# Passing the second chunk of MLP columns for batches 0 and 1 before the third: a reordered opening stage in a fused attention, GLU and soft-MoE kernel

## The chip, the cores and the metric

The kernel runs on one core of a Trainium2 chip. The metric is device time in microseconds of one execution; the median of three runs of the kernel before is 681.73 us (680.27 to 682.89). All times below are microseconds unless marked ns. Engines are named as in the profile: PE is TensorE's matmul side, PEld its weight loads, DVE VectorE, ACT ScalarE, POOL GpSimd, SP the engine that issues nearly all transfers.

## What is computed

Eight batches of 512 rows and 32 state rows each go through a cross read, a gated MLP and a soft mixture of experts:

```python
scores = scale * x @ state.T;  xread = softmax(scores) @ state        # per batch and head
scores2 = scale * state @ x.T; sread = softmax(scores2) @ x
y = concat(xread, sread)                                              # 4352 rows of 512 in all
xn = y / sqrt(mean(y*y) + 1e-6) * rms_g
z = (silu(xn @ w_gate) * (xn @ w_val)) @ w_out                        # 1536 columns inside
logits = z @ phi                                                      # 32 slots
slot_in = softmax(logits, over rows).T @ z
out = softmax(logits, over slots) @ experts(slot_in)                  # 8 experts
```

The inner 1536 columns of the MLP are three chunks of 512, numbered 0, 1 and 2 (`c`). The weights `w_gate`, `w_val` and `w_out` arrive as 64-bit floats and are converted on the chip.

## The kernel before, in words

**Units.** The main work is a list of units (g, c, t): batch g, chunk c, tile t of 128 rows. A unit has two slots. In slot 1 PE makes six matmuls of 128x512 into a bank `mm` for the gate (`main_mm`, line 453), ACT takes their SiLU into `sg` (`main_silu`, line 469); in slot 2 PE makes six more for the value, and DVE multiplies the two into `h` (`main_h`, line 474). Ahead of and behind each slot stand the pieces of work that the table `at(u, slot, f, ...)` (line 800 on) puts there. The units of one stage are written out in `stages` (line 777). Stage 0 has sixteen units: batch 0 chunk 0, batch 1 chunk 0, batch 0 chunk 1, batch 0 chunk 2. Stage 1 has eight: batch 1 chunks 1 and 2. From stage 2 on each stage is one batch with its three chunks.

**Weights.** `w_gate` and `w_val` come in half chunks of 1 MB, then `w_out` transposed in six half chunks of 1 MB, each by one transfer that SP issues (`wload`, line 147, tile `raw` or, for every other late one, `raw_t`, which has a single buffer). Each half chunk is converted in two steps. `begin` (lines 172 and 733) is two ACT passes of 1024 columns (lines 184 and 187). `conv1` (lines 192 and 728) is, for each of two halves of 512 columns, three DVE passes (lines 200, 204 and 208) and one POOL addition (line 212), and then the issue of a further load. The results are the tiles `w` (one for each of gate and value and chunk) and `wo`. A table entry of `begin` or `conv1` always takes the next half chunk in the order of loading, so moving an entry moves all that follow.

**Per batch and chunk.** `sw(b, c, gv)` (line 430) multiplies the state of batch b, scaled by `rms_g`, into the converted weights: eight matmuls of 32 output rows into two `misc` banks; ACT copies each bank into `wp` (line 442) and DVE writes the rounding remainder (line 443). The main matmuls of that batch and chunk read this `wp` and the tile `A` of the batch's attention. Three `misc` banks serve all small work in turn, so a group of matmuls waits until the bank used three groups earlier has been read by ACT and DVE. `att_b1` (line 312) uses two of them for the transposes whose copies are `e2T` (line 318); `att_b2` and `att_b3` make the state read of a batch from it (`srd`, `xsT`).

**Output weights.** `wphi_part(c, j)` (line 624) multiplies `phi` with a converted half chunk `wo`; its second half (lines 635 to 639) finishes `wphi` of chunk c. Only then may the `h` tiles of that chunk be turned (`h_T`, line 484, transposes on L109 and a copy to `hT`) and give logits (`lg_mm`, line 494, tile `lg`).

**Order.** Within a slot the framework's scheduler sets the order of instructions on each engine; each engine then runs its own list strictly in that order, and SP issues its transfers in order too, each behind its waits.

Of the kernel before, what the change touches and what calls it, by code (L numbers as in the profile page):

```python
# [20 lines left out]
def kernel(  # L21
# [17 lines left out]
    B, P, H, NT, D = x_n.shape  # L39
# [734 lines left out]
    def rinv(b):  # L774
        rinv_from(b, T[b, "ss"], NT)

    stages = [
        [(g, c, t) for g, c in ((0, 0), (1, 0), (0, 1), (0, 2)) for t in range(NT)],
        [(1, c, t) for c in (1, 2) for t in range(NT)],
    ]  # L780
    for g in range(2, B):
        stages.append([(g, c, t) for c in range(NC) for t in range(NT)])
# [16 lines left out]
    for s, units in enumerate(stages):  # L799
        def at(u, slot, f, *a):  # L800
            plan.setdefault((base + u, slot), []).append((f, a))

        if s == 0:
# [21 lines left out]
            at(3, 1, att_b2, 0)  # L825
            at(5, 1, att_b3, 0)
            at(4, 1, conv1)
            at(6, 2, begin)
            at(6, 1, conv1)
            at(5, 1, sw, 0, 1, 0)  # L830
            at(6, 2, sw, 0, 1, 1)
            at(5, 2, begin)
            at(5, 2, conv1)
            at(7, 2, begin)
            at(8, 1, conv1)
            at(10, 1, att_b1, 1)
            at(9, 1, begin)
            at(6, 2, conv1)
            at(8, 1, begin)
            at(8, 1, conv1)  # L840
            at(10, 2, sw, 0, 2, 0)
            at(10, 2, begin)
            at(11, 1, sw, 0, 2, 1)
            at(12, 2, conv1)
            at(12, 1, wphi_part, 0, 0)
            at(12, 1, begin)
            at(10, 2, conv1)
            at(12, 2, wphi_part, 0, 1)
            at(11, 2, begin)
            at(12, 2, conv1)  # L850
            at(13, 2, wphi_part, 1, 0)
            at(13, 1, sw, 1, 1, 0)
            at(14, 1, begin)
            at(14, 2, conv1)
            at(14, 2, wphi_part, 1, 1)
            at(14, 1, sw, 1, 1, 1)
            at(14, 1, begin)
            at(15, 2, conv1)
            at(15, 2, wphi_part, 2, 0)
            at(11, 2, load_xn, 1)  # L860
# [5 lines left out]
        else:  # L866
            g = s
# [445 lines left out]
```

## Time and profile before

| | us |
|---|---|
| median of 3 runs | 681.73 (680.27 to 682.89) |
| the profiled execution | 679.36 |
| its span | 677.6 |
| PE busy | 635.2 (94%) |
| DVE busy | 405.3 (60%) |
| ACT busy | 388.2 (57%) |
| POOL busy | 131.1 (19%) |
| TensorE's mean granted clock | 0.973 of full speed |

The profile's page gives busy time by engine, the span in 40 slices, the chain of work that ended last, and groups of instructions with what ended their waits. PE holds 74% of the chain that ended last. The trace's timeline of an engine gives, for each run of like instructions, the start, the time from the first start to the last end, the instruction and its tiles (output <- inputs), the count, and in brackets the idle time ahead of it and what ended it. One matmul of float32 data with 32 output rows shows as two records (so `x16` is one `sw` of eight); a main matmul shows as one.

### The profile page before, as it was taken

To read this page: it belongs to the slowest core of one execution; us is meant where nothing else is said; L and a number is where in the kernel's file an instruction comes from. 1 tells how busy PE (TensorE), PEld (TensorE's weight loads), DVE (VectorE), ACT (ScalarE), POOL (GpSimd) and SP (SyncE) were. 2 spreads that over 40 slices of the span, in tenths; PEclk is the share of its full clock that TensorE was granted. 3 is DMA by queue.
4 is the path that set the end of the run, shared out by engine and by line. 5 is a ranking of instruction groups with operands and counts; after the bars stand their busy time and mean duration, and the time that the engine had idled before them with its cause. 6 is when DMAs were issued, how large, how long until landed. Compare 5 with 4: busy or idle time off the path is not lost.

```text
span 677.6 us, 11521 instructions
## 1 busy us (share of the span) xinstructions
PE 635.2 (94%) x4560; PEld 406.8 (60%) x4560; DVE 405.3 (60%) x852; ACT 388.2 (57%) x632; POOL 131.1 (19%) x158
## 2 busy tenths in 40 slices
PE   5789989999999999999999999999999999999980
PEld 4447646456656766666676667666765776753350
DVE  6979996873676368555835773685465366242170
ACT  5467943855786468557755964685445476311170
POOL 2634656230041102010201021011000000002420
PEclk9599979999999999999999999999999999999996
DMA  9950155031042030203110320300091218999858
GB/s 349 405 211 2 60 189 211 38 133 63 1 160 98 5 124 3 98 5 125 36 63 5 121 94 1 122 4 33 13 359 54 73 39 274 314 340 387 324 196 331
DMA packets 33582, 92.56 MB, mean 137 GB/s; under 512 B 1912, under 2 KB 4088, under 8 KB 30712
## 3 DMA queue, kind: packets, MB, share of 16 engines
q1 hardware_dynamic: 33240, 91.76, 37.1%
q8 instruction: 36, 0.59, 0.4%
q14 instruction: 18, 0.15, 0.1%
q10 hardware_dynamic: 288, 0.07, 0.0%
HBM read 79.76 MB, written 12.06 MB: 136 GB/s over the span
## 4 chain that ended last, share of the span: by engine, by line
PE 74%; DVE 8%; ACT 4%; issue 2%; DVEq 0%; POOL 0%; ACTq 0%
PE mm L85 42%; PE misc L85 17%; PE misc L109 10%; PE lg L85 4%; PE so L85 2%; DVE w L200 1%; DVE wp L443 1%; DVE h L479 1%; DVE w L208 1%; ACT L471 1%; ACT L285 1%; DVE wo L208 1%; ACT sg L471 1%; ACT sT L285 0%; DVE w L204 0%
## 5 line engine op out<-in xcount | busy, mean ns | idle before, releaser
L85 PE MATMUL mm<-wp,A 128*128 128x512 f32 x1152 | 310.6, 408 | 0.4 <-DVE h L479 0.4
L85 PEld LDWEIGHTS mm<-wp,A 128*128 128x128 f32 x1152 | 206.4, 190 | 88.0 <-issue 49.1
L479 DVE SCALAR_TENSOR_TENSOR h<-mm,rinv,sg 128x512 f32<-128x512 f32 x102 | 76.0, 747 | 96.0 <-PE mm L85 73.9
L471 ACT ACTIVATE sg<-mm,rinv 128x512 f32<-128x512 f32 x102 | 70.1, 688 | 74.6 <-PE mm L85 68.3
L442 ACT CAST wp<-misc 128x512 fp32r<-128x512 f32 x96 | 51.9, 587 | 65.0 <-PE misc L85 65.0
L443 DVE TENSOR_TENSOR wp<-misc,wp 128x512 fp32r<-128x512 f32 x96 | 62.2, 684 | 41.1 <-ACT wp L442 40.7
L85 PE MATMUL misc<-w,stTg 64*32 64x512 f32 x768 | 70.0, 618 | 9.6 <-POOL w L212 6.0
L490 ACT COPY hT<-misc 128x512 f32<-128x512 f32 x86 | 49.1, 580 | 24.3 <-PE misc L109 20.0
L109 PE MATMUL misc<-ident,h 128*128 128x128 f32 x408 | 60.4, 274 | 1.8 <-DVE h L479 1.4
L109 PEld LDWEIGHTS misc<-ident,h 128*128 128x128 f32 x408 | 48.9, 140 | 16.9 <-DVE h L479 3.4
L308 POOL TENSOR_TENSOR a<-a,asum 128x1024 f32<-128x1024 f32 x7 | 13.4, 1920 | 126.7 <-DVE asum L307 120.5
L471 ACT ACT_TABLE_LOAD x28 | 35.9, 1283 | 3.1 <-PE mm L85 2.7
L85 PEld LDWEIGHTS misc<-w,stTg 64*32 64x32 f32 x768 | 11.7, 106 | 41.3 <-issue 15.7
L416 POOL TENSOR_TENSOR rinv<-ri,rs_magic 128x4 int32<-128x4 int32 (+1 forms) x9 | 1.8, 197 | 173.8 <-DVE ri L412 173.8
L85 PE MATMUL lg<-hT,wphi 128*32 128x512 f32 (+1 forms) x216 | 32.5, 578 | 1.5 <-ACT hT L490 1.5
L212 POOL TENSOR_TENSOR w<-w,raw 128x512 int32<-128x512 int32 x20 | 28.1, 1419 | 27.6 <-ACT wp L442 7.2
L85 PE MATMUL misc<-bd,A 128*128 128x256 f32 x192 | 31.1, 302 | 1.5 <-DVE A L380 1.5
L85 PE MATMUL mm<-wh,xsg 128*128 128x512 f32 x96 | 31.7, 400 | 0.0
L397 ACT ACTIVATE misc<-misc 128x512 f32<-128x512 f32 x32 | 18.8, 586 | 21.7 <-PE misc L85 20.7
L85 PEld LDWEIGHTS misc<-bd,A 128*128 128x128 f32 x192 | 27.2, 202 | 5.8 <-DVE A L380 2.2
L212 POOL TENSOR_TENSOR wo<-wo,raw 128x512 int32<-128x512 int32 x18 | 24.3, 1362 | 28.4 <-DVE wo L208 19.7
L85 PE MATMUL misc<-h,ET 128*32 128x512 f32 x204 | 28.9, 598 | 0.0
(197 smaller groups left out, 828.2 us busy)
## 6 DMA issues: line engine op xcount, KB each, us to landing
ew<-in_w_dram SPq DMA_DIRECT2D x27, 1024.0 KB, 8.3
xT<-in_x_t_dram SPq DMA_DIRECT2D x8, 1024.0 KB, 4.8
xn<-in_x_n_dram SPq DMA_DIRECT2D x8, 1024.0 KB, 6.9
raw<-in_w_val_dram SPq DMA_DIRECT2D x6, 1024.0 KB, 16.6
raw<-in_w_out_dram SPq DMA_DIRECT2D x6, 1024.0 KB, 5.0
out_dram<-ob SPq DMA_DIRECT2D x6, 1024.0 KB, 12.1
ew_w<-in_w_dram SPq DMA_DIRECT2D x5, 1024.0 KB, 10.2
raw<-in_w_gate_dram SPq DMA_DIRECT2D x4, 1024.0 KB, 14.2
```

The lines of the kernel that those rows point to most:

```text
L85: nc.tensor.matmul(out=o, lhsT=lhsT, rhs=rhs, start=start, stop=stop)
L109: nc.tensor.transpose(o, i, ident)
L200: nc.vector.tensor_scalar(out=dst[:, h], in0=dst[:, h], scalar1=EXP_LO, scalar2=EXP_HI, op0=ALU.max, op1=ALU.min,)
L208: nc.vector.scalar_tensor_tensor(out=a[:, h], in0=hi[:, h], scalar=-0x40000000, in1=a[:, h], op0=ALU.bitwise_and, op1=ALU.bitwise_or,)
L212: nc.gpsimd.tensor_tensor(out=a[:, h], in0=a[:, h], in1=rnd[:, h], op=ALU.add)
L308: (eng or nc.gpsimd).tensor_tensor(out=a3, in0=a3, in1=asum.unsqueeze(2).to_broadcast([P, 32, 32]), op=ALU.mult)
L397: nc.scalar.activation(out=ps, in_=ps, func=AF.Square, accum_out=T[b, "ss"][:, t : t + 1])
L442: nc.scalar.copy(t[:, r, 0, :], ps)
L443: nc.vector.tensor_tensor(out=t[:, r, 1, :], in0=ps, in1=t[:, r, 0, :].bitcast(F32), op=ALU.subtract)
L471: nc.scalar.activation(out=sg, in_=ps, func=AF.Silu, scale=RINV[g][:, t : t + 1])
L479: nc.vector.scalar_tensor_tensor(out=HH[g, c][:, t, :], in0=ps, scalar=RINV[g][:, t : t + 1], in1=sg, op0=ALU.mult, op1=ALU.mult,)
L490: (nc.vector.tensor_copy if on_dve else nc.scalar.copy)(HT[g, c][:, :, t * P : (t + 1) * P], ps.rearrange("p (q n) -> p q n", q=4))
```

## The change

The units of stages 0 and 1 change places: chunk 1 is passed by batch 0 and then batch 1 in stage 0, chunk 2 by batch 0 and then batch 1 in stage 1. The number of units of each stage stays, and so does every instruction of the computation. The table of stage 0 is rewritten from unit 6 on: the state products `sw(1, 1, ...)` come in units 10 and 11 and `sw(0, 2, ...)` in units 13 and 14, where they stood the other way round; the conversions of the third chunk and of the transposed output weights, and the parts of `wphi`, come one to three units later. Everything from stage 2 on is written as before.

```diff
     stages = [
-        [(g, c, t) for g, c in ((0, 0), (1, 0), (0, 1), (0, 2)) for t in range(NT)],
-        [(1, c, t) for c in (1, 2) for t in range(NT)],
+        [(g, c, t) for g, c in ((0, 0), (1, 0), (0, 1), (1, 1)) for t in range(NT)],
+        [(g, 2, t) for g in (0, 1) for t in range(NT)],
     ]
...
-            at(10, 2, sw, 0, 2, 0)
...
-            at(12, 1, wphi_part, 0, 0)
...
+            at(10, 2, sw, 1, 1, 0)
...
+            at(13, 1, wphi_part, 0, 0)
+            at(13, 1, sw, 0, 2, 0)
```

Three places show how instructions move. In the names, `w_4` and `w_5` are the converted gate and value of chunk 2, `wp_6` and `wp_7` the state products for gate and value of the unit that follows unit 11 (batch 0 chunk 2 before, batch 1 chunk 1 now), `wo32` a half chunk of output weights; the last numbers of a name differ between the two programs and mean nothing.

**First place: DVE in units 9 to 12.** Before, on DVE:

```order
L208 SCALAR_TENSOR_TENSOR w_5_776<-raw_9_303,w_5_776 128x512 x2
L479 SCALAR_TENSOR_TENSOR h_2_817<-mm_810,rinv_328,sg_786 128x512
L479 SCALAR_TENSOR_TENSOR h_2_817<-mm_831,rinv_328,sg_826 128x512
L318 COPY e2T_848<-misc_849 128x512
L479 SCALAR_TENSOR_TENSOR h_2_817<-mm_861,rinv_328,sg_846 128x512
L443 TENSOR_TENSOR wp_6_869<-misc_870,wp_6_869 128x512
```

Now, on DVE:

```order
L208 SCALAR_TENSOR_TENSOR w_5_794<-raw_8_253,w_5_794 128x512 x2
L318 COPY e2T_833<-misc_834 128x512
L479 SCALAR_TENSOR_TENSOR h_2_792<-mm_848,rinv_328,sg_831 128x512
L200 TENSOR_SCALAR w_5_794<-w_5_794 128x512 x2
L204 TENSOR_SCALAR w_5_794<-w_5_794 128x512
L443 TENSOR_TENSOR wp_6_856<-misc_857,wp_6_856 128x512
L443 TENSOR_TENSOR wp_6_856<-misc_864,wp_6_856 128x512
L208 SCALAR_TENSOR_TENSOR w_5_794<-raw_9_303,w_5_794 128x512
```

The copy to `e2T` now stands ahead of the last half chunk of `w_5` instead of behind it; of that half chunk, three of the five listed passes stand ahead of the remainders of `wp_6`, and the others behind them.

**Second place: PE from unit 12 on.** Before, on PE, with the third chunk's main matmuls of batch 0:

```order
L85 MATMUL mm_940<-wp_6_869,A_0_255 128x512 x6
L85 MATMUL misc_949<-wo32_828,phis_85 32x512 x2
L85 MATMUL mm_992<-wp_7_906,A_0_255 128x512 x6
L85 MATMUL mm_1034<-wp_6_869,A_0_255 128x512 x6
L85 MATMUL mm_1071<-wp_7_906,A_0_255 128x512 x6
```

Now, on PE, the end of unit 15, of batch 1 in chunk 1:

```order
L85 MATMUL misc_1005<-wo32_890,phis_85 32x512 x2
L85 MATMUL misc_1011<-w_4_736,stTg_147 32x512 x4
L85 MATMUL misc_1018<-w_4_736,stTg_147 32x512 x4
L85 MATMUL misc_1043<-wo32_943,phis_85 32x512 x2
L85 MATMUL mm_1127<-wp_6_856,A_1_456 128x512 x4
L85 MATMUL mm_1179<-wp_7_893,A_1_456 128x512 x5
L85 MATMUL misc_1047<-r32_75,wpp_1008 128x32 x4
```

The first product with output weights (`misc<-wo32`) stood inside unit 12; it now stands in unit 15, beside the first use of `w_4`, and the matmuls with `r32` that finish `wphi` of chunk 0 follow the second product as they did.

**Third place: SP's loads of the transposed output weights.** Before, on SP:

```order
L162 DMA raw_t13_757<-in_w_out_t_dram 128x2x1024
L162 DMA raw_10_796<-in_w_out_t_dram 128x2x1024
L162 DMA raw_11_895<-in_w_out_t_dram 128x2x1024
L118 DMA xT_2_923<-in_x_t_dram 128x2048
L162 DMA raw_t15_808<-in_w_out_t_dram 128x2x1024
L126 DMA xn_1_938<-in_x_n_dram 128x2048
L162 DMA raw_12_1029<-in_w_out_t_dram 128x2x1024
L162 DMA raw_t17_1009<-in_w_out_t_dram 128x2x1024
```

Now, on SP:

```order
L162 DMA raw_t13_783<-in_w_out_t_dram 128x2x1024
L162 DMA raw_10_822<-in_w_out_t_dram 128x2x1024
L118 DMA xT_2_910<-in_x_t_dram 128x2048
L126 DMA xn_1_922<-in_x_n_dram 128x2048
L162 DMA raw_t15_888<-in_w_out_t_dram 128x2x1024
L162 DMA raw_11_941<-in_w_out_t_dram 128x2x1024
L162 DMA raw_t17_1033<-in_w_out_t_dram 128x2x1024
L162 DMA raw_12_1101<-in_w_out_t_dram 128x2x1024
```

The loads of `raw_11` and `raw_12` move behind `raw_t15` and `raw_t17`, each of which waits for POOL's last addition on the `raw_t` half chunk before it, since they share one buffer.

## Rows read from the trace of the kernel before

**Rows 1.** The page, busy time of one engine over the span.

```profile
PE 635.2 (94%) x4560; PEld 406.8 (60%) x4560; DVE 405.3 (60%) x852; ACT 388.2 (57%) x632; POOL 131.1 (19%) x158
```

**Rows 2.** Waits of PE from 40 to 260 us: total, times, longest.

```profile
PE misc L85 <- DVE e2T L318: 3.1, 1, 3.1
```

**Rows 3.** Busy time by stretch: stretch, length, PE, PEld, DVE, ACT, POOL, clock, DMA.

```profile
60.00:91.00 31.00, 30.28 (x227) 20.93 (x226) 29.15 (x59) 25.30 (x37) 17.48 (x13) 1.00 0.27 103
...
95.00:101.00 6.00, 6.00 (x24) 3.05 (x19) 5.79 (x13) 1.17 (x2) 2.68 (x2) 0.50 0.01 3
```

**Rows 4.** Timeline of PE around the wait and the units after it.

```profile
75.54 1.07 PE L85 MATMUL misc<-w,stTg 64*32 64x512 f32 x10 [0.21 <-POOL w L212]
76.54 9.82 PE L85 MATMUL mm<-wp,A 128*128 128x512 f32 x42
...
89.79 1.66 PE L85 MATMUL mm<-wp,A 128*128 128x512 f32 x6
94.53 3.10 PE L85 MATMUL misc<-w,stTg 64*32 64x512 f32 x16 [3.08 <-DVE e2T L318]
97.56 4.78 PE L85 MATMUL mm<-wp,A 128*128 128x512 f32 x12
102.26 1.05 PE L85 MATMUL misc<-wo,phis 128*32 128x512 f32 x4
103.25 8.01 PE L85 MATMUL mm<-wp,A 128*128 128x512 f32 x34
```

**Rows 5.** Timeline of DVE, 79 to 109 us.

```profile
79.76 1.29 DVE L200 TENSOR_SCALAR w<-w 128x512 f32<-128x512 f32 x2
...
83.51 2.32 DVE L200 TENSOR_SCALAR w<-w 128x512 f32<-128x512 f32 x2
...
87.63 2.97 DVE L200 TENSOR_SCALAR w<-w 128x512 f32<-128x512 f32 x2
...
91.19 1.28 DVE L208 SCALAR_TENSOR_TENSOR w<-raw,w 128x512 int32<-128x512 int32 x2
...
93.72 0.67 DVE L318 COPY e2T<-misc 128x512 f32<-128x512 f32 x1
...
94.97 0.67 DVE L443 TENSOR_TENSOR wp<-misc,wp 128x512 fp32r<-128x512 f32 x1
...
108.40 0.75 DVE L200 TENSOR_SCALAR wo<-wo 128x512 f32<-128x512 f32 x2
```

**Rows 6.** Timeline of POOL, one pair of additions.

```profile
82.45 3.09 POOL L212 TENSOR_TENSOR w<-w,raw 128x512 int32<-128x512 int32 x2 [2.03 <-ACT sg L471]
```

**Rows 7.** Timeline of SP, and the DMA issues by line (count, size, us to landing).

```profile
80.88 0.98 SPq L162 DMA_DIRECT2D raw<-in_w_out_t_dram  x2
...
101.55 0.37 SPq L162 DMA_DIRECT2D raw_t<-in_w_out_t_dram  x1
...
raw_t<-in_w_out_t_dram SPq DMA_DIRECT2D x3, 1024.0 KB, 5.0
raw<-in_w_out_t_dram SPq DMA_DIRECT2D x3, 1024.0 KB, 8.1
```

**Rows 8.** Timeline of PE at four later points, and two rates.

```profile
115.34 1.08 PE L85 MATMUL misc<-r,wpp 64*128 64x32 f32 x8 [0.39 <-DVE wpp L635]
...
128.04 1.09 PE L109 MATMUL misc<-ident,h 128*128 128x128 f32 x8
...
139.08 1.07 PE L85 MATMUL misc<-r,wpp 64*128 64x32 f32 x8
...
148.13 1.06 PE L85 MATMUL lg<-hT,wphi 128*32 128x512 f32 x8
...
154.22 1.64 PE L85 MATMUL mm<-wp,A 128*128 128x512 f32 x6
```

**Rows 9.** PE before a second wait early on: timeline row, and clock by stretch.

```profile
12.68 1.12 PE L85 MATMUL misc<-w,stTg 64*32 64x512 f32 x4
...
16.00:16.50 0.50, 0.00 (x0) 0.51 1.01 418
```

More of the change, by code (lines that the diff above doesn't have):

```diff
@@ L827 @@
             at(4, 1, conv1)
-            at(6, 2, begin)
-            at(6, 1, conv1)
             at(5, 1, sw, 0, 1, 0)
             at(6, 2, sw, 0, 1, 1)
-            at(5, 2, begin)
             at(5, 2, conv1)
-            at(7, 2, begin)
+            at(6, 2, begin)
+            at(7, 1, conv1)
+            at(7, 1, begin)
             at(8, 1, conv1)
+            at(8, 2, begin)
+            at(9, 2, conv1)
             at(10, 1, att_b1, 1)
[L837 to L840, printed above, removed]
-            at(10, 2, sw, 0, 2, 0)
-            at(10, 2, begin)
-            at(11, 1, sw, 0, 2, 1)
-            at(12, 2, conv1)
-            at(12, 1, wphi_part, 0, 0)
-            at(12, 1, begin)
[L847 to L853, printed above, removed]
+            at(10, 1, begin)
+            at(10, 2, sw, 1, 1, 0)
+            at(11, 1, conv1)
+            at(11, 1, begin)
+            at(11, 1, sw, 1, 1, 1)
+            at(12, 1, conv1)
+            at(12, 1, begin)
+            at(12, 2, begin)
+            at(13, 1, wphi_part, 0, 0)
+            at(13, 1, sw, 0, 2, 0)
+            at(13, 1, conv1)
+            at(13, 2, wphi_part, 0, 1)
+            at(13, 2, begin)
+            at(14, 1, sw, 0, 2, 1)
+            at(14, 1, conv1)
+            at(14, 2, wphi_part, 1, 0)
+            at(14, 2, begin)
             at(14, 2, conv1)
-            at(14, 2, wphi_part, 1, 1)
-            at(14, 1, sw, 1, 1, 1)
-            at(14, 1, begin)
+            at(15, 1, wphi_part, 1, 1)
+            at(15, 1, begin)
             at(15, 2, conv1)
```

## The prediction, made before the change was run

> **What bounds the kernel now.** I began with busy time: PE works 635.2 of 677.6 us [rows 1], so only time in which PE stands still, or runs at its lower clock, can be won. PE's waits show where: between 40 and 260 us one wait stands out, 3.08 us for DVE's copy to `e2T` [rows 2]. PE's timeline places it: the main matmuls end near 91.4, and the `sw` that follows (0, 2, value) begins at 94.53 [rows 4]. The stretches give its cause and its tail. DVE is busy 29.15 of 31 us ahead of it, with the conversion of the third chunk; and from 95 to 101 the granted clock is 0.50, TensorE's 1.2 GHz level [rows 3], after 3.08 us without a matmul. Twelve main matmuls take 4.7 us there, 0.39 each, against 8.01 / 34 = 0.235 afterwards [rows 4]. So about 7 us at most hang on this place: 3.1 of waiting and some 3.5 of slow clock. All else in these stages runs nearly full, with 0.39 us ahead of one `wphi` step [rows 8]. About 0.5% of the time, 3.4 us, is what a measurement of this kernel can tell from no change.
>
> **The change, part by part.** No instruction is added or removed, so the sum is made of waits.
>
> *The first wait moves two groups on.* In the new order only the first half chunk of `w_5` stands ahead of the `e2T` copy. Laid out from where the orders part, that copy ends near 91.5, just as PE arrives. But the second group of the next `sw` needs the bank that the first remainder of `wp_6` frees, and that remainder stands behind three passes of the last half chunk. Before, it ended at 94.97 + 0.67 = 95.64 [rows 5]. Three things shift it:
> - Two L208 and one L204 pass now come after it: 2 x 0.64 from the L208 pair, and 0.38, half of the free L200 pair, which L204 equals [rows 5]: -1.65.
> - DVE now reaches the remainders of `wp_5` with no conversion ahead of them. Their second group's matmuls run from 75.54 to 76.61 [rows 4], ACT's copies come behind those, and ACT's passes for the next half chunk behind the copies. DVE, which had no pause here, stands still about 2.1 (bounds 0, if something fills it, and 3.1, the longest wait that PE's rows show): +2.1.
> - L200 takes 0.75 for a pair when POOL is idle, and 1.29, 2.32 and 2.97 when a pair of POOL's additions (3.09 [rows 6]) is under way [rows 5]. With a fourth pair like the first that is 4.9 over the free price. Now one pair starts with POOL idle, and three start some 1.1 before POOL ends: 3.4. That gives -1.5.
>
> Sum -1.05: the remainder ends near 94.6, and PE resumes at about 94.8, having done four of the eight `sw` matmuls and waited 2.2 in place of 3.08. Its next main matmuls start at 94.8 + 1.07 = 95.9 where they started at 97.56 [rows 4]: **1.65 ahead**, if the clock stays up.
>
> The L200 rows ask for a rule. The pair begun at 83.51 ends at 85.83, 0.3 after the POOL pair that began before it [rows 5, 6]. The Trainium skill (SBUF — State Buffer, "Who interferes with whom") says that VectorE in a two-port mode and GpSimd hold a shared port pair exclusively, whichever issues first, and the other blocks fully; the rows agree. Were the two engines independent, the three pairs would cost 0.75 each, the remainder would come 3 us sooner, the wait of 2.2 would close and the sum would be 679.3; by the rule it is the one below. I take the blocked price because three rows of three show it.
>
> *A second wait opens at unit 12.* The remainders of `wp_7` stand behind three L208, three L204 and two L200 passes (1.9 + 1.1 + 0.75 = 3.8) that follow `wp_6`'s second remainder (95.3). With 0.9 for POOL in the way (between 0 and 2.2, the dearest pair [rows 5]) the first `wp_7` remainder ends near 100.7. PE gets through the `sw` and twelve matmuls by 98.7, issues one of the next six and waits until 100.9: **2.0 us** (1.1 to 3.3). Before, that point of unit 12 was passed at 103.25 + 0.23, so the change is 2.5 ahead. But the first output-weight product, 1.05 [rows 4], was done by then and is now still to come: **1.5 ahead**. So DVE, not the clock, now sets this stretch; most of what the slow clock cost is spent again as waiting.
>
> *The output weights.* Two of the first three half chunks were issued as a pair at 80.88 and landed long before use; `raw_t15` went at 101.55 [rows 7]. Now `raw_11` stands behind `raw_t15`, which waits for POOL's last addition on the first half chunk, whose last L208 stands behind `wp_7`: near 104.1. It lands 5.0 later [rows 7], at 109.2 (8.1, the other rows' landing, is the upper bound). ACT's two passes then hold up its copies for `wp_8`, and the `wphi` sum on DVE ends near 115.0. PE waits about 1.0 and reaches the `r32` step at 115.1, against 115.34 [rows 8]. By then it has also done one `sw` and a transpose that before came later, 1.3 together: still **1.5 ahead**. At the same place the covers go: conversions that ran 3 to 20 us ahead of their products now end as PE arrives. Every product waits for POOL's addition just behind DVE's last pass, and one L208 stands behind the `wphi` copy of the chunk before. By the order I count waits of 1.4, 1.0, 2.2, 0.8, 1.3 and 0.6 up to the last `r32` step, which PE reaches near 140.6 against 139.08 [rows 8]. It has then done 15 more main matmuls (3.5) and eight fewer transposes and four fewer logits matmuls (about 1.85 by [rows 8]; a group of eight transposes or four logits matmuls is 1.06 to 1.09): 1.65 more work, so only **0.1 ahead**.
>
> *Until the orders meet.* `xn_1`, `xT_2` and `xT_3` have 5 us and more in hand after the move. ACT swaps its tables once more in this stretch, beside PE's matmuls; I cost that at nothing; if the SiLUs behind a swap came due, it is in the 1 either way below. The next stage's first main matmuls of batch 1 chunk 2 I place at 151.6 with 2.45 of small work left over, 154.05 against 154.22 [rows 8]. From there the lists carry the same work, and I take 0, with 1 either way.
>
> **Sum:** 0.2 less, on a profiled execution of 679.36. That execution is 2.4 below the median of 681.73; the difference is laid on the median: **681.5 us**.
>
> **The rivals.**
>
> *The hole closes (faster).* If DVE comes to `wp_6` by 92.3 and to `wp_7` by 98.7, 2 us sooner than I count, nothing waits, the clock stays at 2.4 GHz, and what remains to pay is only the output weights' 1.4. For it: each of my DVE terms has bounds of that size, and the conversion does come later. Against it: DVE's queue still holds all four half chunks' passes but two. Price: 3.08 + 3.5 for the hole, less 1.4: 676.5; without that 1.4, 675.2.
>
> *The clock falls twice (slower).* Near 13.8 the `sw` matmuls end and the granted clock is 0.51 by 16.0 [rows 9]: 2.2 us without a matmul sufficed there. So the wait for `wp_6` (2.2) and the wait for `wp_7` (2.0) may each put PE down to 1.2 GHz. The first fall is nearly free, since DVE sets the next stop anyway (0.7). The second falls on unit 12 to 15, which DVE does not hold, and costs 3.5 as the fall before did. It decides at the wait for `wp_7`, whose upper bound is 3.3. Price: 681.5 + 4.2 = 685.7. Against it: four `sw` matmuls split the first wait, and 2.0 is shorter than what both rows show. The Trainium skill (TensorE: Matmul & The Clock Gate, "HAM oscillation — how this bites in real kernels") says that waits between bursts put the clock down again each time, which speaks for this rival; that the single wait of before cost one fall agrees.
>
> *Late loads (slower).* If `raw_t15` and `raw_t17` land after 8.1 instead of 5.0 [rows 7], ACT's strict order holds SiLUs and copies behind them, twice 3.1 less the 2 us of slack that I left: 4.2 more, 685.7.
>
> *The change does nothing (same).* If the scheduler had kept `e2T` behind the conversion, the time would stay at 681.7; the order shows that it did not.
>
> **How the numbers follow.** My forecast, that the wait moves and the output weights give back the rest, gets 0.5. The closed hole gets 0.24, the double fall 0.15, late loads 0.09, and no effect 0.02, which adds to same. So faster 0.24, same 0.52, slower 0.24. The forecast's own range by its bounds (wait for `wp_7` 1.1 to 3.3, pause 0 to 3.1, one either way at the end) is 679 to 684. To leave out no more than 2 in 10 it reaches to the closed hole that still pays for the output weights and to both slow cases: **676.5 to 686**.
>
> **What would show it.** Right: no wait of PE on `e2T` worth naming; a wait of about 2 us on DVE `wp` L443 near 93 and another near 100; a granted clock that stays at 1.00 from 91 to 104; PE waits on POOL `wo` L212 and on DVE `wpp` and `wphi` adding up to 5 to 8 us between 115 and 140; the issue of `raw_t15` near 104. Wrong: PE without waits over 1 us from 91 to 104 (the closed hole), a clock of 0.50 in that stretch or behind it (the double fall), or an ACT wait on the transfer to `raw_t` of more than 4 us (late loads).

## The result, and the profile after

The changed kernel takes **686.15 us** (median of 5 runs, 685.64 to 686.43) against 681.0 for the kernel before in the same session (5 runs): a ratio of **1.0087 [1.0071, 1.0103]**, so slower by 5 to 6 us. The forecast was 681.5, no change that could be told, with a range to 686.0. The profiled execution took 685.64 for a span of 683.8, where before had 677.6, so the two traces differ by 6.2; before's is one of its faster executions (679.36, median 681.0).

The page's busy time of one engine (answers [rows 1]): PE works 3 us more, which no added work explains.

```profile
PE 638.3 (93%) x4560; PEld 405.1 (59%) x4560; DVE 409.3 (60%) x854; ACT 390.8 (57%) x632; POOL 128.0 (19%) x158
```

PE's waits from 40 to 280 us (answers [rows 2]; columns: total, times, longest):

```profile
PE misc L85 <- DVE wp L443: 2.3, 1, 2.3
PE misc L85 <- POOL wo L212: 2.2, 3, 1.5
...
PE misc L85 <- DVE e2T L318: 0.5, 1, 0.5
```

The wait for `e2T` shrank from 3.1 to 0.5 and one for `wp` took its place, as forecast. The waits for POOL's `wo` are new; the forecast had them, and larger. The stretches (answer [rows 3]; columns as there):

```profile
91.00:95.00 4.00, 1.30 (x10) 0.15 (x8) 4.00 (x7) 3.26 (x5) 2.52 (x2) 0.91 0.77 268
95.00:101.00 6.00, 5.87 (x18) 3.34 (x18) 5.96 (x10) 0.59 (x1) 2.76 (x2) 0.50 0.40 164
...
116.00:140.00 24.00, 21.55 (x124) 10.96 (x124) 19.58 (x38) 15.46 (x23) 8.39 (x7) 1.00 0.24 88
```

From 95 to 101 the clock is 0.50, as before. From 116 to 140 PE stands still 2.45 us, where before had 0.29 (11.77 + 11.94 busy in the two halves of that stretch). PE's timeline (answers [rows 4] and [rows 8]):

```profile
91.76 1.06 PE L85 MATMUL misc<-w,stTg 64*32 64x512 f32 x8 [0.52 <-DVE e2T L318]
95.13 1.93 PE L85 MATMUL misc<-w,stTg 64*32 64x512 f32 x8 [2.31 <-DVE wp L443]
...
116.36 1.07 PE L85 MATMUL misc<-r,wpp 64*128 64x32 f32 x8 [0.28 <-DVE wpp L635]
...
119.77 1.05 PE L85 MATMUL misc<-wo,phis 128*32 128x512 f32 x4
...
122.61 1.05 PE L85 MATMUL misc<-wo,phis 128*32 128x512 f32 x2
...
126.11 1.43 PE L85 MATMUL mm<-wp,A 128*128 128x512 f32 x5
...
127.46 1.07 PE L85 MATMUL misc<-r,wpp 64*128 64x32 f32 x8
...
131.03 1.04 PE L85 MATMUL misc<-wo,phis 128*32 128x512 f32 x2 [1.47 <-POOL wo L212]
...
132.94 1.05 PE L85 MATMUL misc<-wo,phis 128*32 128x512 f32 x2 [0.21 <-POOL wo L212]
...
137.56 1.05 PE L85 MATMUL misc<-wo,phis 128*32 128x512 f32 x2 [0.49 <-POOL wo L212]
...
142.15 1.04 PE L85 MATMUL misc<-wo,phis 128*32 128x512 f32 x2
...
144.95 1.08 PE L85 MATMUL misc<-r,wpp 64*128 64x32 f32 x8
...
156.66 1.65 PE L85 MATMUL mm<-wp,A 128*128 128x512 f32 x6
```

Two things are to be seen. First, a product of the output weights that stands whole (x4, at 119.77) takes 1.05; cut in two (x2 and x2, at 131.03 and 132.94, and at 137.56 and 142.15) each half takes as long as the whole, 1.04 to 1.05, and from the start of one to the next row on PE pass 0.97 or 0.98. That is about 1 us for each of these two. A third product is cut together with the logits matmuls beside it: from 122.61 to 126.11 the two take 3.50. In before they took 1.84 (122.54 to 124.38), and one product alone ran long, 2.03:

```profile
122.54 1.07 PE L85 MATMUL lg<-hT,wphi 128*32 128x512 f32 x8
123.42 1.03 PE L85 MATMUL misc<-wo,phis 128*32 128x512 f32 x4
124.38 2.56 PE L85 MATMUL mm<-wp,A 128*128 128x512 f32 x9
...
135.06 2.03 PE L85 MATMUL misc<-wo,phis 128*32 128x512 f32 x4
```

The cuts are busy time, and no view of waits shows them. Second, how the halves come about, in the changed kernel's rows of DVE and POOL behind the `r32` step of 127.46:

```profile
128.57 0.29 DVE L639 COPY wphi<-misc 128x128 f32<-128x128 f32 x1 [1.83 <-PE misc L85]
128.78 0.68 DVE L208 SCALAR_TENSOR_TENSOR wo<-raw_t,wo 128x512 int32<-128x512 int32 x1
```

```profile
129.69 1.28 POOL L212 TENSOR_TENSOR wo<-wo,raw_t 128x512 int32<-128x512 int32 x1 [5.48 <-PE misc L85]
131.60 1.29 POOL L212 TENSOR_TENSOR wo<-wo,raw_t 128x512 int32<-128x512 int32 x1 [0.63 <-DVE wo L208]
```

PE's `r32` step releases DVE's copy, which had kept DVE still for 1.83; behind it in DVE's order stands the L208 pass of the next half chunk, behind that POOL's addition, and behind that PE's product, which starts at 131.03 after 1.47 of waiting. (The row names PE's step as what ended POOL's idle time; the addition reads what L208 wrote, and that ended at 129.46.) PE waits for work that waited for PE.

Where the 6.2 us arise, by the prediction's places: at the first `r32` step (116.36) the kernel was about 0.3 ahead (1.02 later, with 1.3 more work done); at the last (144.95) 4.2 behind (5.87 later, 1.65 more done); at unit 20 (156.66, with 2.45 of work left over) 4.9 behind; at the end 6.2.

### The profile page after: what moved, and what is told of

Read it like the earlier page. It is cut to its first block, busy times and chain, and to the rows that moved or that the text cites. A ratio compares the mean times of both kernels' runs of the same rounds, so it can differ in the third digit from the quotient of the medians.

```text
span 683.8 us, 11523 instructions
## 1 busy us (share of the span) xinstructions
PE 638.3 (93%) x4560; PEld 405.1 (59%) x4560; DVE 409.3 (60%) x854; ACT 390.8 (57%) x632; POOL 128.0 (19%) x158
## 4 chain that ended last, share of the span: by engine, by line
PE 73%; ACT 6%; DVE 6%; issue 2%; POOL 1%; DVEq 0%; ACTq 0%; POOLq 0%
PE mm L85 41%; PE misc L85 17%; PE misc L109 9%; PE lg L85 4%; PE so L85 2%; ACT L471 1%; DVE w L200 1%; ACT L285 1%; ACT sg L471 1%; ACT sT L285 1%; DVE wp L443 1%; DVE wo L208 1%; ACT hT L490 1%; DVE h L479 1%; ACT wp L442 0%
## 5 line engine op out<-in xcount | busy, mean ns | idle before, releaser
L479 DVE SCALAR_TENSOR_TENSOR h<-mm,rinv,sg 128x512 f32<-128x512 f32 x102 | 75.8, 745 | 91.7 <-PE mm L85 73.9
L443 DVE TENSOR_TENSOR wp<-misc,wp 128x512 fp32r<-128x512 f32 x96 | 62.5, 684 | 41.0 <-ACT wp L442 40.4
## 6 DMA issues: line engine op xcount, KB each, us to landing
raw<-in_w_gate_dram SPq DMA_DIRECT2D x4, 1024.0 KB, 14.2
```

What stands on the lines that cost most here:

```text
L443: nc.vector.tensor_tensor(out=t[:, r, 1, :], in0=ps, in1=t[:, r, 0, :].bitcast(F32), op=ALU.subtract)
L479: nc.vector.scalar_tensor_tensor(out=HH[g, c][:, t, :], in0=ps, scalar=RINV[g][:, t : t + 1], in1=sg, op0=ALU.mult, op1=ALU.mult,)
```

## The experiments

The traces do not start alike. The fourth `h` pass (DVE L479), ahead of everything that any edit moves, begins at 61.83 in before and in the changed kernel, but between 61.70 and 63.68 in the others. A single span is therefore compared after taking that difference off. That is the last column. For two kernels there is a second trace (order_timed, late_wo_timed); by it the column would read +1.2 and about +6 instead of +0.6 and +5.5, so it is good to some 0.6 us.

| run | span | fourth `h` | against before |
|---|---|---|---|
| before | 677.6 | 61.83 | 0 |
| the change | 683.8 | 61.83 | +6.2 |
| order_alone | 678.3 | 61.98 | +0.6 |
| late_wo_alone | 684.5 | 63.21 | +5.5 |
| early_wo | 685.9 | 61.94 | +8.2 |
| early_wo_xn | 685.6 | 61.81 | +8.0 |
| products_later | 679.6 | 62.31 | +1.5 |
| pool_whole | 687.0 | 61.80 | +9.4 |
| late_products | 683.5 | 61.98 | +5.8 |
| late_products_b3 | 680.6 | 61.82 | +3.0 |
| wp_first | 684.0 | 61.77 | +6.5 |
| begin8_later | 689.1 | 61.79 | +11.5 |
| both_later | 680.1 | 61.92 | +2.4 |
| both_later_b3 | 682.1 | 63.42 | +2.9 |
| both_latest_b3 | 684.1 | 61.76 | +6.6 |
| before_e2t_act | 679.5 | 62.87 | +0.9 |
| order_e2t | 680.5 | 63.68 | +1.0 |
| before_e2t_pool | 682.0 | 61.70 | +4.5 |

### Which half of the change costs

**order_alone** takes before's table and changes the order of units and the two pairs of `sw` alone:

```diff
-        [(g, c, t) for g, c in ((0, 0), (1, 0), (0, 1), (0, 2)) for t in range(NT)],
-        [(1, c, t) for c in (1, 2) for t in range(NT)],
+        [(g, c, t) for g, c in ((0, 0), (1, 0), (0, 1), (1, 1)) for t in range(NT)],
+        [(g, 2, t) for g in (0, 1) for t in range(NT)],
...
-            at(10, 2, sw, 0, 2, 0)
+            at(10, 2, sw, 1, 1, 0)
```

> Part 1 of the change alone: the units and the two pairs of scaled weights change places, every conversion and every product of the output weights stays at the unit where the kernel before has it. Theory W (the 6.2 us come from the later conversions): span 676.5 to 678.5, as before's 677.6, and the last r32 step near 139 to 140. Theory O (they come from the new order of the units itself): span 682.5 to 684.5 as after's 683.8.

**late_wo_alone** keeps before's order and its conversions of the gate and value columns, and moves the output weights alone:

```diff
-            at(12, 2, conv1)
-            at(12, 1, wphi_part, 0, 0)
+            at(12, 1, conv1)
...
+            at(13, 1, wphi_part, 0, 0)
...
-            at(14, 2, wphi_part, 1, 1)
...
+            at(15, 1, wphi_part, 1, 1)
```

> The kernel before with its order of units and its conversions of the gate and value columns, but with the six output-weight conversions, their beginnings and their products at the units where the change has them. Theory W: the loss of the stretch 116 to 145 comes here too, 3.5 to 5 us, span 681 to 683, and TensorE again waits some 2 us for POOL wo. Theory O: span 677 to 678.5.

The section on the change says that these pieces come one to three units later. For the output weights the table moves less: the first three conversions come half a unit to one and a half later and the first four products half a unit to one, while the last three conversions and the last two products keep their slots and only their beginnings come later.

Measured: +0.6 and +5.5, together 6.1 of the change's 6.2; the second is a little over what theory W gave. Both were timed again, in five rounds each.

> The new order of units with before's conversions and products, timed in five rounds beside the kernel before. By the traces 0.55 us over before when the starts are made equal: ratio 1.000 to 1.002. If the order has a larger part that the single trace hid: 1.003 or more.

> Before's order with the output weights' conversions and products where the change has them, timed in five rounds. By the traces 5.5 us over before when the starts are made equal: ratio 1.007 to 1.009. If one trace overstated it: 1.005 or less.

Ratios: **1.0009 [0.9998, 1.002]** for the order, **1.0075 [1.0062, 1.0087]** for the late output weights. Theory W is shown, theory O falls: the order of units is worth nothing that a measurement can tell, the later output weights are the loss. The two PE timelines show it too; first late_wo_alone, with the change's halves and waits, then order_alone, with before's one cut product:

```profile
132.63 1.04 PE L85 MATMUL misc<-wo,phis 128*32 128x512 f32 x2 [1.47 <-POOL wo L212]
134.55 1.05 PE L85 MATMUL misc<-wo,phis 128*32 128x512 f32 x2 [0.22 <-POOL wo L212]
139.16 1.04 PE L85 MATMUL misc<-wo,phis 128*32 128x512 f32 x2 [0.48 <-POOL wo L212]
143.77 1.04 PE L85 MATMUL misc<-wo,phis 128*32 128x512 f32 x2
146.57 1.08 PE L85 MATMUL misc<-r,wpp 64*128 64x32 f32 x8
```

```profile
134.94 2.03 PE L85 MATMUL misc<-wo,phis 128*32 128x512 f32 x4
...
138.95 1.07 PE L85 MATMUL misc<-r,wpp 64*128 64x32 f32 x8
```

### What in the late output weights costs

**early_wo** is the changed kernel with five of the six conversions half a unit earlier and the six beginnings half a unit to a unit earlier; **early_wo_xn** moves the load of `xn_1` ahead of them as well.

```diff
+            at(10, 2, begin)
+            at(11, 1, sw, 1, 1, 1)
+            at(11, 2, conv1)
             at(11, 1, begin)
-            at(11, 1, sw, 1, 1, 1)
-            at(12, 1, conv1)
...
```

> The changed kernel with its new order, and its six output-weight conversions half a unit to a unit earlier; the products stay, so each finds its weights converted. Theory W: the POOL wo wait of 2.2 us goes and 3 to 4.5 of the 6.2 us come back, span 679 to 681. Theory O: span 683 to 684.5, within half a us of the changed kernel.

```diff
+            at(10, 1, load_xn, 1)
...
-            at(11, 2, load_xn, 1)
```

> The run early_wo (span 685.9) with the load of batch 1's xn put ahead of the output weights' loads on the queue, where early_wo left TensorE waiting 3.3 us for it. Theory W (early weights are what the change gave away): the wait for xn goes, and with it the second fall of the clock; span 679 to 681.5. Rival (VectorE is the bound up to 108 and the wait only changes its name): 683 to 685.

Measured: +8.2 and +8.0, two misses. In early_wo the waits for POOL `wo` are gone, but the transfer of `xn_1` now stands behind the output weights' loads:

```profile
114.59 1.10 PE L85 MATMUL misc<-xn,e2T 128*32 128x64 f32 x64 [3.30 <-DMA xn<-in_x_n_dram]
117.38 0.48 PE L109 MATMUL misc<-ident,srd 128*128 128x128 f32 x1 [1.69 <-DVE srd L339]
```

With `xn_1` ahead that wait goes too, and nothing comes back: PE waits for `wp` at other places instead (2.4 us in two waits on L443 between 104 and 150, the longer 1.8, beside the 2.3). DVE is busy 13.00 of 13 us from 91 to 104 in both; a conversion put earlier there takes its place in a queue that has no gap. So "earlier is better" is false as well.

**products_later** leaves the change's conversions and moves the products and `r32` steps behind them, half a unit to a unit:

```diff
-            at(13, 1, wphi_part, 0, 0)
...
-            at(13, 2, wphi_part, 0, 1)
...
+            at(13, 2, wphi_part, 0, 0)
+            at(14, 2, wphi_part, 0, 1)
...
-                at(0, 2, wphi_part, 2, 1)
+                at(0, 2, wphi_part, 2, 0)
+                at(1, 1, wphi_part, 2, 1)
```

> The changed kernel with its conversions where they are, and the six products half a unit to a unit later still, so that none stands in the middle of its conversion. Theory L: the 2.2 us of waits for POOL wo and most of the half products (about 0.5 us each, five of them) go, so 3.5 to 4.5 us come back: span 679 to 680.5. Theory T: span 684 to 686, later than the changed kernel.

Measured: +1.5, so 4.7 of the 6.2 come back, more than theory L gave. Every product is whole and none waits for POOL, so the run takes away waits and cuts together and does not price them apart; its PE timeline at the last two:

```profile
136.63 1.02 PE L85 MATMUL misc<-wo,phis 128*32 128x512 f32 x4
...
141.66 1.05 PE L85 MATMUL misc<-wo,phis 128*32 128x512 f32 x4
...
143.99 1.07 PE L85 MATMUL misc<-r,wpp 64*128 64x32 f32 x8
```

**pool_whole** keeps the change's table and replaces POOL's two additions on an output-weight half chunk by one:

```diff
-                nc.gpsimd.tensor_tensor(
-                    out=a[:, h], in0=a[:, h], in1=rnd[:, h], op=ALU.add
-                )
+                if gv != 2:
+                    nc.gpsimd.tensor_tensor(
+                        out=a[:, h], in0=a[:, h], in1=rnd[:, h], op=ALU.add
+                    )
             if gv == 2:
+                nc.gpsimd.tensor_tensor(out=a, in0=a, in1=rnd, op=ALU.add)
```

> The changed kernel with its whole table, but each output-weight conversion ends in one GpSimd addition of 128x1024 in place of two of 128x512, so that no product can begin on half of its weights. Theory L in its narrow form (the half products cost about 0.5 us each, four or five of them, beside 2.2 us of waits): the products stand whole again, 2 to 3 us come back or more if a wait goes too: span 679.5 to 682. Rival (the halves only look long, their time is a wait under another name that now shows as waits for POOL wo): span 683 to 685 and the waits for POOL wo grow by 2 us or more.

Measured: +9.4, 3.2 worse than the change. The half products are gone, and the waits grew (in this kernel the lines behind the edit carry numbers higher by two):

```profile
PE misc L85 <- POOL wo L217: 3.9, 3, 1.9
...
PE misc L85 <- DVE wpp L637: 1.3, 1, 1.3
```

One addition of 128x1024 takes 2.4 to 2.6, one of 128x512 mostly 1.28 to 1.31, so the first half of the weights comes at least 1.1 later, and behind both L208 passes. The waits for POOL `wo` are 1.7 longer than the change's and the one for `wpp` 1.0, about what the three cut products cost. The granted clock is lower too, where the change had 1.00 (pool_whole, 116 to 128 and 128 to 140):

```profile
116.00:128.00 12.00, 9.99 (x58) 4.76 (x61) 10.09 (x18) 8.27 (x11) 4.82 (x2) 0.86 0.48 175
128.00:140.00 12.00, 10.09 (x60) 5.72 (x53) 8.38 (x16) 5.12 (x7) 2.39 (x1) 0.86 0.00 1
```

So the narrow form of theory L falls: whole products at the same place bring nothing back, since PE then waits for the weights instead. What a cut costs by itself this run does not show, since longer waits and a slower clock came with the whole products. With products_later it points at the place of the product rather than its cutting. (In before_e2t_pool the same edit on the kernel before costs 3.6 over before_e2t_act; at most 1 was expected.)

**late_products** asks whether lateness itself costs. It is order_alone, conversions as before, with the first four products where the change has them:

```diff
-            at(12, 1, wphi_part, 0, 0)
...
-            at(12, 2, wphi_part, 0, 1)
...
+            at(13, 1, wphi_part, 0, 0)
+            at(13, 2, wphi_part, 0, 1)
```

> The new order of units with before's conversions (as the run order_alone, span 678.3), and only the first four products of the output weights moved to the units where the change has them. Theory L (the loss lies in products that catch a conversion in the middle: waits for POOL wo and products cut in two): the weights are ready long before, no wait, span 677.5 to 679. Theory T (products that come later are the loss themselves, since transposes and logits pile up behind them): span 681 to 684.

Measured: +5.8, so 5.2 more than order_alone. Theory L, which had no loss here, missed; theory T's number came, though products_later, with products later still, had spoken against its reason. In order_alone the first two products (102.14 and 111.98) and an `r32` step (115.22) stand ahead of the transposition of `srd`, which then waits for nothing. Here they stand behind it:

```profile
114.91 0.33 PE L109 MATMUL misc<-ident,srd 128*128 128x128 f32 x1 [1.85 <-DVE srd L339]
...
117.82 1.05 PE L85 MATMUL misc<-wo,phis 128*32 128x512 f32 x4 [0.58 <-DVE wp L443]
...
125.79 0.49 PE L85 MATMUL mm<-wp,A 128*128 128x512 f32 x1 [1.02 <-ACT wp L442]
```

DVE's pair of L200 ahead of `srd` takes 2.98 in place of 0.76, beside a pair of POOL:

```profile
110.41 2.98 DVE L200 TENSOR_SCALAR wo<-wo 128x512 f32<-128x512 f32 x2
```

```profile
110.02 3.08 POOL L212 TENSOR_TENSOR wo<-wo,raw_t 128x512 int32<-128x512 int32 x2 [3.65 <-ACT wo L184]
```

So PE has nothing to do just where DVE is late. **late_products_b3** tests that: the `srd` transposition, which nothing needs before the last group, goes from 12.2 to 14.2.

> The run late_products (span 683.5, 5.2 over order_alone) with the transposition of srd two units later, which nothing needs before the last group. Theory F (the early products were the work that covered TensorE's wait for srd, 1.85 us, and the VectorE step slowed there): the wait goes and 1.5 to 3 us come back, span 680.5 to 682. Theory T (each unit by which transposes and logits start later is paid whatever waits there are): span 683 to 684.

Measured: +3.0, so 2.8 of the 5.2 come back, as theory F said. The other 2.4 lie in no single wait; they stay open, and with them whether lateness has a price of its own.

### Can the hole of 91 to 104 be closed?

**wp_first** puts the last gate and value conversion behind the second `sw` of (1, 1); **begin8_later** also puts its beginning (ACT's two passes) there, and with it the first output-weight beginning and conversion half a unit later.

```diff
-            at(11, 1, conv1)
             at(11, 1, begin)
             at(11, 1, sw, 1, 1, 1)
+            at(11, 2, conv1)
```

> The changed kernel with one conversion (the last of the value columns' third chunk) moved behind the scaled weights for which TensorE waits at 92.8. Theory C (that wait and the half clock after it cost most): no wait over 1 us there, the clock stays at its upper level to 104, and the span falls by 4 to 6 us to 678 to 680. Rival (VectorE, without a gap from 79 to 108, is the bound there): the 2.3 us go but come back as later waits for conversions, span 682 to 684.

```diff
-            at(10, 1, begin)
             at(10, 2, sw, 1, 1, 0)
-            at(11, 1, conv1)
+            at(12, 1, conv1)
+            at(11, 1, sw, 1, 1, 1)
             at(11, 1, begin)
-            at(11, 1, sw, 1, 1, 1)
-            at(12, 1, conv1)
+            at(11, 2, begin)
+            at(12, 2, conv1)
```

> The changed kernel, with the beginning of the last gate and value conversion behind the second pair of scaled weights, so that its VectorE steps no longer stand ahead of the subtraction that TensorE waits for at 92.8. Theory C (that wait of 2.3 us and the half clock of 95 to 101 cost): the wait falls under 0.5 us, the clock stays up, and the end comes 2.5 to 5 us earlier, span 679 to 681.5. Theory D (VectorE is full from 79 to 108 and hands the wait on to the next conversion, as in wp_first): span 683 to 684.5.

wp_first: +6.5, and the wait of 2.31 stays. The edit did not reach the instructions: PE's order and DVE's around this place are those of the change, so neither theory was tested and this trace is in effect a second execution of the change. In it the clock was up again earlier (0.81 from 98 to 101, where the first had 0.50), and PE spent what it won on a wait of 1.07 for `wp` that ended at 101.91: the slow clock is free there. begin8_later: +11.5, far over what either theory gave. The wait does go and the clock stays at 1.00 to 104; then PE stands 3.6 us before the `srd` transposition, and the clock falls there. What the other half unit in this edit cost was not separated. **both_later** joins this to products_later, **both_later_b3** moves the `srd` transposition to 14.2, and **both_latest_b3** the products half a unit to a unit later again.

> The last two edits together. If both L and C hold and add, span 675.5 to 677.5, at or under before's 677.6; with L alone 679 to 680.5; with neither 683 or more.

> The run both_later (span 680.1; there TensorE ran at the full clock through 91 to 104 and then waited 3.6 us for srd, after which the clock fell) with srd's transposition two units later. If that wait is the whole price, the span falls by 3.6 and some 1.5 for the clock to 675 to 677, under before's 677.6. Rival: the first product of the output weights stands next in TensorE's order and waits in its place for its conversion: span 679 to 681 and a wait for POOL wo of 2 us or more near 105.

> The last edit with the output weights' products a unit later again, so that none waits for its conversion near 105. Theory F: no wait over 1 us between 91 and 140, span 674.5 to 677. Theory T, or the queue of h tiles that wait for their products grows until loads find no room: span 679 or more.

Measured: +2.4, +2.9, +6.6. Moving the products takes 9.1 off begin8_later, more than the 4.7 that it took off the change; the edits at the hole win nothing on top of products_later (+1.5). The stretches of both_later:

```profile
91.00:104.00 13.00, 12.24 (x119) 8.04 (x117) 12.19 (x22) 9.23 (x11) 6.51 (x5) 1.00 0.63 239
104.00:116.00 12.00, 8.38 (x47) 1.99 (x46) 10.50 (x19) 5.77 (x7) 6.44 (x5) 0.72 0.52 177
```

The hole is there, 12 us later. In both_later_b3 the wait for `srd` stays too (3.8), now ahead of the first product and probably through the bank that the step frees; neither its theory nor its rival had that. On the kernel before, **before_e2t_act** gives batch 1's `e2T` to ACT alone; **order_e2t** does so on order_alone; **before_e2t_pool** joins the first to pool_whole's edit.

```diff
-            (nc.scalar.copy if r else nc.vector.tensor_copy)(
+            (nc.scalar.copy if r or b == 1 else nc.vector.tensor_copy)(
```

> The kernel before with one copy moved: batch 1's e2T, for which TensorE waits 3.1 us at 91.4, goes wholly to ScalarE, which is idle there, and not behind three VectorE conversions. Theory C (that wait and the half clock behind it are paid in full): TensorE goes on at about 92.2 at the upper clock, span 672.5 to 675. Theory D (VectorE's conversions are the bound there; the wait moves to the scaled weights or to h): less than 1.5 us, span 676 to 677.6.

> The new order with before's conversions (order_alone, 678.3) and batch 1's e2T copied by ScalarE alone. In before_e2t_act TensorE then waited for POOL w 1.3 us, for weights of the third chunk; in this order the next scaled weights use columns converted long before, so TensorE goes on at 92.2 for at least the first eight products. Theory D (VectorE is the bound to 104): the wait moves to the scaled weights, span 676.8 to 678.5. Theory C: 674 to 676.5.

> The last edit, with the one GpSimd addition for each output-weight conversion as in pool_whole, on the kernel before. There one product of its six is cut in two and another runs 0.45 us long, so this adds at most 1 us to what the last run gives: span 671.5 to 677.

Measured: +0.9, +1.0, +4.5. PE no longer waits for `e2T`, but 1.3 for POOL `w` in the first and this, from the waits of order_e2t, in the second:

```profile
PE misc L85 <- DVE wp L443: 3.8, 1, 3.8
```

In before_e2t_act and order_e2t theory C, which gave a gain of about 2 us or more, misses; theory D gave a little less than was measured. Of the eight kernels with an edit at this hole wp_first changed nothing there; in the other seven a wait of 1.3 to 3.8 us came again at the next step that DVE, or POOL behind it, owes, and the end came no earlier than 0.9 after before's. That speaks for theory D, DVE's queue as the bound from 79 to 108, but does not show it: a kernel with less DVE work there was not tried. No version tried beats the kernel before.

## Why the prediction was wrong

*The first wait moves two groups on: right.* PE waits 0.52 for `e2T` and 2.31 for `wp_6` (2.2 said), and resumes at 95.13 (94.8). DVE's pause was 1.63 (2.1 said). The four L200 pairs took 0.76, 2.34, 1.81 and 1.85, 3.8 over the free price against 3.4. Without those 3.8, by the same sum, the wait of 2.31 would have closed; no run tests that. The Trainium skill (SBUF — State Buffer, "Who interferes with whom") says that of VectorE in a two-port mode and GpSimd the one that issues first holds the shared port pair for its whole instruction and blocks the other fully; these rows and the pair of 2.98 in late_products agree.

*"If the clock stays up": it did not.* It fell in the moved wait, to 0.50 from 95 to 101. It cost next to nothing, as the prediction's own sentence "DVE, not the clock, now sets this stretch" has it: the second wait of 2.0 for `wp_7` was simply not seen, since a slow PE came as late as DVE, and wp_first, with the clock up earlier, reached the first `r32` step at 116.3 too. The rivals of the double fall and of the late loads both priced 685.7 and so came close to the time, but not for their reasons: there was one fall, and it was free, and the loads took no longer than before.

*The output weights: the step that failed.* The prediction made them cost 1.4: from 1.5 ahead to "only 0.1 ahead" at the last `r32` step. They cost 5.7: from the 1.5 to 4.2 behind.
- Its own waits are not in its sum. It counts waits of 1.4, 1.0, 2.2, 0.8, 1.3 and 0.6 "up to the last `r32` step", 7.3 together (6.3 if the 1.0 is the one ahead of the first `r32` step), and its signs say 5 to 8. But it puts the two `r32` steps at 115.1 and 140.6, 25.5 apart, and the work in between is 23.8: 23.74 between the same steps of before, less 0.29 of idle time, and 0.35 more work (1.65 less the 1.3 done ahead). That leaves 1.7 for all waits, or 2.7 with before's one cut product priced whole. With 6.3 to 7.3 in it the last step would stand at 144.2 to 146.2 and the sum at 685.1 to 687.1; measured were 144.95 and 686.15. So close a hit would have been luck in part, for the waits were not of that size, as the next points show.
- 1.2 of the loss came ahead of the first `r32` step, at 116.36 and not 115.1: `raw_t15` was issued at 105.35, not 104.1, since POOL's last addition on the buffer ended at 105.3. It landed 5.0 later, as [rows 7] said. ACT did wait 4.68 for the transfer, which the prediction had named as a sign of late loads; the transfer was not late, its issue was.
- 4.5 came from there to 144.95. The places of the waits were right (POOL `wo`, DVE's L208 behind the `wphi` copy), the sizes not: 2.2 of idle time between the two steps, where before had 0.3. The other part is the cutting, which was not priced: each product went in at 1.05, from the one row that shows it whole. The three cut products took 0.97, 0.97 and (with the logits) 1.66 more than whole ones, against 0.98 for before's one. 1.9 more waiting and 2.6 more in cut products make the 4.5.

*Until the orders meet, and after: "I take 0, with 1 either way".* It was 0.7 up to unit 20 and 1.3 after it. The later waits (two for `wp` of 0.6, one for ACT's `hT` of 0.5) stand in order_alone too, so they belong to the order of units; that run ends only 0.6 behind before, so it won some of it back elsewhere.

*The chances.* Within 0.5% got 0.52, slower by more 0.24. The mechanism that cost the time was in the prediction, conversions that end as PE arrives; its price was not in the sum. And the list held waits alone, while the loop through PE, DVE and POOL took more in cut products than in waits.

## What to carry to other kernels

When a list of waits is part of a forecast, check that the places given hold work and waits together. When a producer moves close to its consumer, price the consumer as cut at each boundary that the producer works in, and read the order of instructions for the cuts: time lost in halves counts as busy, and no list of waits shows it. Move such a pair together and leave the consumer its distance: with both late and the products moved a further half unit to a unit, 4.7 of 6.2 us came back. Distance alone is not enough: with the conversions early and the products late (late_products) nothing was won, since a wait elsewhere lost its cover. Work that seems to wait for no one may be what an engine does while another is late, and where one engine's queue is full, taking away a wait moves it to the next step that the engine owes.

## What the runs showed that was not expected

- The two halves of an output-weight product take 1.04 and 1.05 one by one and 1.05 together, so the second half is free when both are ready. Both are of 128x32 shape and write different partitions of one bank. The Trainium skill (TensorEngine Tiling (Array Packing), "Key Properties") says that different tiles of the array can execute weight loads and matmuls in parallel; the rows agree, and no run here tried another layout.
- The length of a wait does not tell alone whether the clock falls. In late_products a wait of 1.85 ending at 114.91 left it at 1.00; in pool_whole it fell to 0.50 by 120 behind a wait of 1.31 that ended at 117.46.
- The start of the traces differs by up to 2 us between kernels that are the same up to there (fourth `h` pass at 61.70 to 63.68), about half of the spread of before's runs (679.16 to 682.89). Its cause was not looked at.
